# Seven products instead of eight for four pairs of f tiles of the first half, with sums on GpSimd and gated sums added by DMA

## The chip, the cores and the metric

The kernel runs on one core of a Trainium2 chip. The metric is device time in microseconds of one execution, the median of several runs. Beside it stands one profiled execution with its trace. The engines are named as in the profile: PE is the matmul engine and PEld its weight loads, DVE the vector engine, ACT the scalar engine, POOL is GpSimd, SP issues most DMAs. Each engine takes its instructions in the order of its own list; an instruction that waits for another engine holds up what stands behind it in the same list.

## The reference

A token matrix x (2048 x 512) goes through two branches that a gate mixes:

```python
g = sigmoid((x * gate_w).sum(-1, keepdims=True))
a = irfft2(rfft2(x) * (w_r + 1j * w_i))            # 2048 x 512, filter in the frequency domain
h = gelu(x @ w1 + b1)                              # 512 -> 1792
b = h @ w2 + b2                                    # 1792 -> 512
return g * a + (1 - g) * b
```

All of it is fp32. The kernel gets fp32 accuracy from the fast matmul format by splitting each operand into a high and a low part: a product takes three matmuls (high x high, high x low, low x high).

## The kernel before

**Tiling.** The tokens are four groups `c` of 512, the hidden width is 14 tiles `f` of 128, the model width 4 tiles `q` of 128. Groups 0 and 1 (`CA`) are the first half, 2 and 3 (`CB`) the second.

**First half.** `mlp(p, c)` runs three passes over f, `PASS_A = 0-4, 5-9, 10-13`. For each f and group it makes `ph = w1[f] x` (L916, 12 matmuls of 512 columns: four q, three for the split), applies gelu in PSUM on ACT (L904), splits the result into `g_..h` (ACT, L466) and `g_..l` (DVE, L467), and then `down` (L961) makes, for each q, `po = w2 g`, three matmuls for each f tile. `keep` (L971) copies `po` out on ACT with the sign turned and writes it to the DRAM tensor `bacc[c]`: plainly in the first pass, with an accumulating DMA from POOL (`acc`, L407) in the later ones. Weights that are not summed are split as `h` on ACT; the low part is made as minus `h` (ACT, L472) plus an accumulating DMA of the weight (POOL, L407).

**Second half.** `fast(p)` (L1070), four passes, `PASS_B = 0-3, 4-5, 6-9, 10-13`. It takes the f tiles in pairs and the two groups together as a 2 x 2 block product, by a scheme with seven products instead of eight (seven `times` calls of six matmuls, L1090). The scheme needs sums of weight halves (`spread_w`, L1032: `sub` makes four 128x256 sums for each pair on DVE, L1051; `sums` splits the results into high and low, L1047 and L1048) and sums of token tiles (`early_x` and `spread_x`, L1006 and L1018: `less`, L994, 128x512, on DVE; `put` splits them, L990 and L991). Products go to two PSUM banks `nu` of each pair and to two banks `ux` that are held for good; copies and additions between them run on ACT (`copy`, L1096) and DVE (`plus`, L1099). Results are split and multiplied down as in the first half, with `+1.0` in `keep`.

**The end.** In the last pass of the second half, `bacc` is read back into `bb`, multiplied by gate - 1 (L1140), and subtracted on DVE from the filter branch in the tile `y` (L1144, two 128x256 for each block). `last` (L1156) then subtracts the last down product from `y` into `oB` (L1171) and sends it out; the block that closes the kernel is cut into pieces (`tail`, L1164 for the last one), so that the last DMAs are small.

**The filter branch** runs beside all this: forward transforms (`forward`, matmuls `pd` and `py`) in the first 90 us or so, butterflies and the filter product on DVE (`radix4`, L665 to L669; `filt`, L765 to L769) after them, inverse transforms (`inverse`, `pz` and `pa`) in the last 130 us. `own_rows` sends some rows of `y` through a DMA and a small matmul before the second stage of butterflies can start.

**Order.** Every step is recorded in a graph, and two tables written out by hand or by a planner set everything: `ORDER` is the order in which the steps are emitted, and so each engine's list, and `SLOTS` is the buffer slot of each tile.

Of the kernel before, what the change touches and what calls it, by code (L numbers as in the profile page):

```python
# [16 lines left out]
P = 128  # L17
# [6 lines left out]
PASS_A = (range(0, 5), range(5, 10), range(10, 14))  # L24
# [321 lines left out]
def tile_kernel(ctx: ExitStack, tc: tile.TileContext, xt, xc, w1, w2, b1, b2, x0g, wf, wrev, out, consts):  # L346
# [9 lines left out]

    vec, act, pe, sp = nc.vector, nc.scalar, nc.tensor, nc.sync

    slots = {"t2k": 7, "ttab": 3, "xhl": 8, "w": 46, "pf": 4, "pm": 4}

    whole = ("ttab", "xhl", "w", "ctab")
    g = Graph(slots)
# [20 lines left out]
    def c_act(n, psum):  # L383
        return 0.07 + 0.82e-3 * n if psum else 0.13 + 0.765e-3 * n
# [894 lines left out]
```

## Time and profile before

| | us |
|---|---|
| median of 3 runs | 365.27 (364.29 to 366.5) |
| the profiled execution | 364.17 |
| its span in the trace | 362.3 |
| POOL busy in the span | 70.6, 91 instructions |
| granted PE clock | 1.0 all through |

The span is what the trace holds of that execution; 1.9 us lie around it. In a row of a group, the two numbers behind the first bar are the busy time of all its instructions and the mean duration of one in ns; behind the second bar stands the engine's idle time just before them and what ended it. A busy PE is one that has matmuls in flight: they overlap, so the time from start to start is less than the 390 ns that a 512-column matmul lasts.

### The profile page before, as it was taken

How to read it: one execution, taken by the hardware profiler on the slowest of the kernel's cores; microseconds unless marked ns; L12 is line 12 of the kernel's file. 1: busy time of each engine (PE TensorE's matmuls, PEld its weight loads, DVE VectorE, ACT ScalarE, POOL GpSimd, SP SyncE). 2: the span in 40 equal slices, each digit the busy share in tenths (PEclk: the TensorE clock that was granted, in tenths of full speed). 3: DMA queues.
4: the chain of work that ended last, by engine and by line, in shares of the span. 5: the costliest groups of instructions: out<-in, count | busy, mean ns of one | idle time of the engine just before them, and what ended most of it. 6: DMA issues, size and time to landing. Idle time of an engine off the chain costs nothing.

```text
span 362.3 us, 5722 instructions
## 1 busy us (share of the span) xinstructions
PE 356.1 (98%) x1808; PEld 302.2 (83%) x1808; DVE 330.8 (91%) x745; ACT 253.6 (70%) x471; POOL 70.6 (19%) x91
## 2 busy tenths in 40 slices
PE   8999999999999999999999999999999999999995
PEld 6988898898877888888888888888888888888885
DVE  5969999799978999999999999979989899899994
ACT  4984688789985563348468764899999986786100
POOL 1030000111021240111224300000432222003220
PEclk9999999999999999999999999999999999999999
DMA  7999597377689899897998954445686588858787
GB/s 242 369 337 263 176 322 203 102 162 184 208 147 237 199 261 211 198 342 226 217 263 152 148 113 134 103 133 166 83 146 123 85 149 208 166 164 203 168 228 221
DMA packets 46494, 70.34 MB, mean 194 GB/s; under 512 B 5376, under 2 KB 19200, under 8 KB 46464
## 3 DMA queue, kind: packets, MB, share of 16 engines
q1 hardware_dynamic: 34592, 48.93, 41.5%
q0 software_dynamic: 11440, 20.72, 37.1%
q10 hardware_dynamic: 432, 0.33, 0.3%
q8 instruction: 14, 0.23, 0.3%
q14 instruction: 16, 0.13, 0.1%
HBM read 48.32 MB, written 19.41 MB: 187 GB/s over the span
## 4 chain that ended last, share of the span: by engine, by line
PE 85%; DMA 5%; DVE 4%; ACT 3%; SPq 1%; issue 1%; DVEq 0%
PE poB L416 21%; PE po L416 20%; PE ph L416 14%; PE ux L1090 10%; PE nu L1090 8%; PE pz L416 4%; PE pd L416 3%; PE py L416 3%; PE pa L416 3%; DMA wb1l<-in_w 2%; DMA wb1l_raw<-in_w 2%; DMA y<-ownr 1%; ACT ph L904 1%; DVE b0s L665 0%; SPq L893 0%
## 5 line engine op out<-in xcount | busy, mean ns | idle before, releaser
L904 ACT ACTIVATE ph<-ph,b1t 128x512 f32<-128x512 f32 x28 | 18.4, 656 | 17.9 <-PE ph L416 17.8
L803 ACT ACTIVATE sw<-y,al 64x512 f32<-64x512 f32 x32 | 22.9, 721 | 1.2 <-DVE y L669 0.5
L407 POOL DMA_DIRECT2D bacc<-oB x16 | 13.9, 936 | 47.1 <-ACT oB L982 46.1
L407 POOL DMA_DIRECT2D bacc<-o x16 | 15.6, 977 | 35.8 <-ACT o L982 35.5
L765 DVE TENSOR_TENSOR m<-y,wf 128x514 f32<-128x514 f32 x32 | 21.3, 691 | 0.3
L982 ACT ACTIVATE o<-po 128x512 f32<-128x512 f32 x16 | 9.5, 596 | 15.4 <-PE po L416 9.9
L416 PEld LDWEIGHTS pz<-tg,pq 128*128 128x128 f32 x128 | 17.1, 191 | 1.9 <-PE pz L416 0.4
L416 PE MATMUL pz<-tg,pq 128*128 128x128 f32 x128 | 17.8, 275 | 0.3 <-DVE v L855 0.3
L416 PE MATMUL pd<-cf,w 128*128 128x129 f32 x128 | 17.7, 274 | 0.0
L1090 PE MATMUL nu<-xf,wa0h 128*128 128x512 f32 x56 | 17.4, 392 | 0.0
L416 PE MATMUL py<-zb,tf 128*128 128x258 f32 x96 | 17.3, 297 | 0.0
L416 PEld LDWEIGHTS pd<-cf,w 128*128 128x128 f32 x128 | 16.6, 190 | 0.6
L607 DVE TENSOR_TENSOR zb<-pd,zb 128x256 fp32r<-128x256 f32 x32 | 13.1, 419 | 4.1 <-ACT zb L604 2.2
L632 ACT ACTIVATE y<-pys 64x257 f32<-64x257 f32 x32 | 13.1, 417 | 3.5 <-DVE pys L629 3.0
L810 DVE SCALAR_TENSOR_TENSOR pq<-y,al,sw 128x256 f32<-128x256 f32 x32 | 14.9, 483 | 0.6 <-ACT sw L806 0.5
L416 PEld LDWEIGHTS pa<-zb,ci 128*128 128x128 f32 x96 | 13.7, 188 | 1.4
L416 PEld LDWEIGHTS py<-zb,tf 128*128 128x128 f32 x96 | 14.1, 190 | 0.9
L416 PE MATMUL pa<-zb,ci 128*128 128x256 f32 x96 | 14.3, 281 | 0.0
L822 ACT ACTIVATE zb<-pz 128x512 fp32r<-128x512 f32 x16 | 9.4, 597 | 6.5 <-PE pz L416 6.4
L604 ACT ACTIVATE zb<-pd 128x256 fp32r<-128x256 f32 x32 | 11.2, 387 | 3.5 <-PE py L416 2.2
L823 DVE TENSOR_TENSOR zb<-pz,zb 128x512 fp32r<-128x512 f32 x16 | 11.0, 691 | 2.8 <-ACT zb L822 2.8
L574 DVE TENSOR_TENSOR w<-eo 128x256 f32<-128x256 f32 x32 | 13.1, 421 | 0.3
(700 smaller groups left out, 1279.9 us busy)
## 6 DMA issues: line engine op xcount, KB each, us to landing
wf<-in_wf SPq DMA_DIRECT2D x16, 257.0 KB, 4.9
bacc<-o POOLq DMA_DIRECT2D x16, 256.0 KB, 7.0
bacc<-oB POOLq DMA_DIRECT2D x16, 256.0 KB, 4.2
xf<-in_xt SPq DMA_DIRECT2D x14, 256.0 KB, 4.9
wr<-in_w SPq DMA_DIRECT2D x14, 256.0 KB, 5.0
tf<-tf SPq DMA_DIRECT2D x16, 192.0 KB, 5.1
bacc<-o SPq DMA_DIRECT2D x8, 256.0 KB, 3.8
bacc<-oB SPq DMA_DIRECT2D x8, 256.0 KB, 2.2
```

The lines of the kernel that those rows point to most:

```text
L407: return add("pool", 2.3 * kb / 340, 3.4, lambda: nc.gpsimd.dma_start(dst(), src(), accum_op=ALU.add), reads, writes, rank)
L416: pe.matmul(ps, w, x, start=start, stop=stop)
L574: v(lambda s=s, op=op: vec.tensor_tensor(w.ap()[:, s], eo.ap()[:, :, 0], eo.ap()[:, :, 1], op=op), 256, [eo], [(w, s)], feed)
L604: a(lambda c=c: act.activation(segs(xh, c), both(c), AF.Copy), 256, [ps[c]], [(xh, c)], 0)
L607: v(lambda c=c: vec.tensor_tensor(segs(xl, c), both(c), segs(xh, c), op=ALU.subtract), 256, [ps[c], (xh, c)], [(xl, c)], 0)
L632: a(lambda o=o, i=i: act.activation(Y[j].ap()[o:o + HP, 1], pys.ap()[i:i + HP, 1], AF.Copy), 257, [(pys, 1)], [(Y[j], 1 + k)], 0, more=0.1)
L765: v(lambda mk=mk, k=k, y=y, w=w: vec.tensor_tensor(mk.ap(), y.ap(), w.ap()[:, k:k + 1, :ND].to_broadcast([P, 2, ND]), op=ALU.mult), 514, [ ...
L803: a(lambda sw=sw, y=y, o=o, i=i: act.activation(sw.ap()[o:o + HP], y.ap()[i:i + HP, ::-1, :HD], AF.Copy, scale=al.ap()[i:i + HP, 0:1]), 51 ...
L810: v(lambda sw=sw, pq_=pq_, y=y, j=j, k=k, op=op: vec.scalar_tensor_tensor(pq_.ap()[:, k], y.ap()[:, k, :HD], al.ap()[:, 1 + j:2 + j], sw.a ...
L823: v(lambda n=n, ps=ps: vec.tensor_tensor(zl.ap()[:, :, :, n], ps.ap(), zh.ap()[:, :, :, n], op=ALU.subtract), 512, [ps, (zh, n)], [(zl, n) ...
L904: a(lambda: act.activation(ps.ap(), ps.ap(), AF.Gelu_apprx_tanh, bias=b1t.ap()[:, f:f + 1]), 600, [b1t], [ps]).table = "gelu"
L1090: pe.matmul(o.ap(), w(wi, e), FX[j].ap()[:, xi, e], start=first, stop=k == 5, skip_group_check=not start)
```

## The change

Four things are done.

- The first half's passes become 0-5, 6-9, 10-13. The first is still `mlp`. The other two are `fast_a`, which uses the seven products, now a function `products` for both halves, on the pairs (6,7), (8,9), (10,11), (12,13). For the first half three of the token operands are the tiles that are there already (`tokens`, `WHOLE`), and only four sums are made. The two PSUM banks `ux` are set up by two matmuls with a tile of zeros.
- All sums of token tiles (`less`) and of weight halves (`sub`) are made by GpSimd, 16 of 128x512 and 44 of 128x256, instead of DVE. The tokens of both halves are loaded whole; a detour of two tiles through DRAM goes.
- At the end `bb` times gate - 1 is added to `y` by an accumulating DMA, eight of them, instead of 16 subtractions on DVE; the sign in `keep` is turned for it.
- `ORDER` and `SLOTS` are new throughout; there are 42 instead of 46 slots of 2 KB and 9 instead of 8 of 8 KB.

By instructions: PE 24 fewer of 512 columns and 2 more, DVE 23 fewer, ACT 24 more, POOL 60 sums more and 4 DMAs fewer for weights and 8 more for `y`, SP as many DMAs as before.

```diff
-PASS_A = (range(0, 5), range(5, 10), range(10, 14))
+PASS_A = (range(0, 6), range(6, 10), range(10, 14))
...
 ORDER = """
-13 0 2 3 4 5 6 7 8 9 10 11 12 15 38 14 16 26 25 506 508 18 507 527 109 1 37 39 27 19 64 17 511 23 554 543 530 167 509
+15 13 0 2 3 4 5 6 7 19 8 9 10 11 12 22 14 16 25 1 26 482 27 23 484 18 24 503 17 38 192 37 483 64 39 65 541 20 552 485
...
-    slots = {"t2k": 7, "ttab": 3, "xhl": 8, "w": 46, "pf": 4, "pm": 4}
+    slots = {"t2k": 7, "ttab": 3, "xhl": 9, "w": 42, "pf": 4, "pm": 4}
...
+    def on_pool(emit, n, reads, writes):
+        return add("gp", c_pool(n), 0.2, emit, reads, writes)
...
     def less(o, x, y):
-        v(lambda: vec.tensor_tensor(o.ap(), x.ap(), y.ap(), op=ALU.subtract), 512, [x, y], [o])
+        on_pool(lambda: nc.gpsimd.tensor_tensor(o.ap(), x.ap(), y.ap(), op=ALU.subtract), 512, [x, y], [o])
...
+    def spread_x(cs, half, after=()):
+
+        raw_ = cs == CB
+        new_forms(("11", "t1", "t2", "21", "t3", "22", "t4") if raw_ else ("t1", "t2", "t3", "t4"), half)
...
+            less(b00, b01, b00)
+            put("t1", e, b00)
             less(b01, b11, b01)
             put("t3", e, b01)
+            if raw_:
+                put("22", e, b11)
+            less(b11, b11, b00)
+            put("t2", e, b11)
+            if raw_:
+                put("21", e, b10)
+            less(b10, b10, b11)
+            put("t4", e, b10)
+
+    WHOLE = {"11": (0, 0), "21": (0, 1), "22": (1, 1)}
+
+    def tokens(half, k):
+        if half == "A" and k in WHOLE:
+            c, n = WHOLE[k]
+            bs = X[CA[c]]
+            return [*bs], lambda i, e: bs[i].ap()[:, :, 2 * n + e]
+        b = FX[k]
+        return [b], lambda i, e: b.ap()[:, i, e].rearrange("p (a b) -> p a b", a=4)
...
         def sub(o, oh, x, xh, y, yh, op=ALU.subtract):
-            v(lambda: vec.tensor_tensor(o.ap()[:, H[oh]], x.ap()[:, H[xh]], y.ap()[:, H[yh]], op=op), 256, [x, y], [o])
+            on_pool(lambda: nc.gpsimd.tensor_tensor(o.ap()[:, H[oh]], x.ap()[:, H[xh]], y.ap()[:, H[yh]], op=op), 256, [x, y], [o])
...
+    def products(half, fs, late, end):
+        cs = CA if half == "A" else CB
+        G = {}
+        if not UX:
+            zero = buf("w", [P, P], F32R, "zerob", cls="zero")
+            add("vec", 0.3, 0.1, lambda: vec.memset(zero.ap().bitcast(F32), 0.0), [], [zero])
+            UX.extend(buf("pm", [P, 512], F32, f"ux{k}", pool=pp, cls=f"ux{k}") for k in range(2))
+            for x in UX:
+                m(lambda x=x: mm(x.ap(), zero.ap(), bcast(zero.ap(), 4), True, True), 512, 1, [zero], [x])
...
+    def fast_a(p):
+        fs = PASS_A[p]
+        G = products("A", fs, [], False)
+        for f in fs:
+            load_w("b", f)
+        for n, c in enumerate(CA):
...
+                down(ps, slice(None), q, fs, W, {f: G[n, f] for f in fs})
+                keep(c, q, o, ps, False, -1.0)
...
-                    for h in range(2):
-                        y = Y[c + 8 * h + 4 * (q // 2)]
-                        v(lambda b=b, y=y, h=h, q=q: vec.tensor_tensor(
-                            y.ap()[:, q % 2, :2 * P], y.ap()[:, q % 2, :2 * P], b.ap()[:, 2 * h * P:2 * (h + 1) * P], op=ALU.subtract),
-                          256, [b], [(y, q % 2)])
+                    j = c + 4 * (q // 2)
+                    acc(lambda j=j, q=q: yy.ap()[:, j::8, q % 2, :2 * P], lambda b=b: b.ap().rearrange("p (a b) -> p a b", a=2), 256,
+                        [b], [(Y[j], q % 2), (Y[j + 8], q % 2)])
...
-                        keep(c, q, o, ps, p == 0, 1.0)
+                        keep(c, q, o, ps, p == 0, -1.0)
...
-    early_x()
-    for p in range(len(PASS_A)):
-        for c in CA:
-            mlp(p, c)
+    for c in CA:
+        mlp(0, c)
+    spread_x(CA, "A")
+    for p in range(1, len(PASS_A)):
+        fast_a(p)
```

Three places in the order that this makes. First, POOL's list where the weights of the first half's second pass are prepared. Before, it holds the accumulating DMAs for the low parts of single weights:

```order
L407 DMA wa10l<-in_w 128x512
L407 DMA wa6l<-in_w 128x512
L407 DMA wa9l<-in_w 128x512
L407 DMA wa7l<-in_w 128x512
L407 DMA wa8l<-in_w 128x512
L407 DMA wb6l<-in_w 128x512
```

In the change the same place holds the sums of weight halves (`wr` are the loaded weights of a pair, `ws` the sum tile), and the DMAs stand between them:

```order
L1060 TENSOR_TENSOR wsA_1098<-wrA_495 128x256
L1060 TENSOR_TENSOR wsA_1098<-wsA_1098,wrA_629 128x256
L1060 TENSOR_TENSOR wrA_495<-wrA_629,wrA_495 128x256
L1060 TENSOR_TENSOR wrA_495<-wrA_629,wsA_1098 128x256
L417 DMA wb6l<-in_w 128x512
L417 DMA wa0lA_1204<-in_w 128x512
L417 DMA wa0lA_1259<-in_w 128x512
L1060 TENSOR_TENSOR wsA_1291<-wrA_808 128x256
L1060 TENSOR_TENSOR wsA_1291<-wsA_1291,wrA_926 128x256
```

Instructions of computing have come into a list that had DMA issues alone.

Second, POOL's list in the second half of the change, where partial results (`oB`) are accumulated into `bacc`:

```order
L417 DMA bacc_2649<-oB_23_3005 128x512
L417 DMA bacc_2649<-oB_22_3083 128x512
L1060 TENSOR_TENSOR wrB_2389<-wrB_2312,wrB_2389 128x256
L417 DMA bacc_2649<-oB_21_3113 128x512
L1060 TENSOR_TENSOR wsB_3136<-wrB_2361 128x256
L1060 TENSOR_TENSOR wrB_2389<-wrB_2312,wsB_2645 128x256
L417 DMA bacc_2649<-oB_20_3190 128x512
```

Sums of weight halves stand behind DMA issues that wait for ACT's copy of a down product.

Third, the end of DVE's list. Before:

```order
L1144 TENSOR_TENSOR y<-y,bb_3923 128x256
L1171 TENSOR_TENSOR oB_32_4168<-y,poB_320_4123 128x256
L1171 TENSOR_TENSOR oB_33_4187<-y,poB_330_4170 128x256
L1144 TENSOR_TENSOR y<-y,bb_4033 128x256
L1164 TENSOR_TENSOR oB_33_4187<-y,poB_33256_4189 128x128 x2
```

and in the change:

```order
L1205 TENSOR_TENSOR oB_30_4178<-y,poB_300_4067 128x256
L1205 TENSOR_TENSOR oB_33_4213<-y,poB_330_4195 128x256
L1205 TENSOR_TENSOR oB_31_4237<-y,poB_310_4221 128x256 x2
L1198 TENSOR_TENSOR oB_33_4213<-y,poB_33256_4206 128x128 x2
L1205 TENSOR_TENSOR oB_20_4264<-y,poB_200_4251 128x256 x2
```

The block cut into small pieces is no longer the last; a whole block, `oB_20`, comes behind it.

More of the change, by code (lines that the diff above doesn't have):

```diff
@@ L381, in c_vec, with c_pool @@
         return 0.075 + 1.042e-3 * n
+    def c_pool(n):
+        return 0.3 + 2.1e-3 * n
     def c_act(n, psum):
@@ L951, in mlp @@
             G[f] = split(f"g{c}_{f}", "w", [P, 512], ps, lambda x: x, 512, cls="g")
-        if p == len(PASS_A) - 1:
-            free[c] = G[fs[-1]][1]
         for q in range(NQ):
@@ L988, in put @@
     def put(k, e, x):
-        h, l = ((lambda i=i: FX[k].ap()[:, i, e]) for i in range(2))
+        b = FX[k]
+        h, l = ((lambda i=i: b.ap()[:, i, e]) for i in range(2))
         a(lambda: act.activation(h(), x.ap(), AF.Copy), 512, [x], [(FX[k], e)])
@@ L993, in less @@
     def less(o, x, y):
-        v(lambda: vec.tensor_tensor(o.ap(), x.ap(), y.ap(), op=ALU.subtract), 512, [x, y], [o])
-    def new_forms(ks):
-        FX.update((k, buf("xhl", [P, 2, 2, 4 * P], F32R, f"xf{k}", parts=4, cls="xf")) for k in ks)
-    def raw_x(k, n, e, tag, cls, after=()):
-        x = buf(tag, [P, 4 * P], F32, f"xb{k}{n}{e}{cls}", cls=cls)
-        dma(lambda: sp.dma_start(x.ap(), xc[CB[n], 2 * k + e]), 256, after, [x])
-        return x
-    t2s = [one(f"t2s{e}", [P, 4 * P], pool=dp) for e in range(2)]
@@ L1006, in early_x @@
-    def early_x():
-        new_forms(("11", "t1", "t2"))
-        for e in range(2):
-            b00, b01, b11 = (raw_x(k, n, e, "w", "xe") for k, n in ((0, 0), (0, 1), (1, 1)))
-            put("11", e, b00)
-            less(b01, b01, b00)
-            put("t1", e, b01)
-            less(b11, b11, b01)
-            put("t2", e, b11)
-            dma(lambda e=e, b11=b11: sp.dma_start(t2s[e].ap(), b11.ap()), 256, [b11], [t2s[e]])
-    def spread_x():
-        new_forms(("21", "t3", "22", "t4"))
-        for e in range(2):
-            b10, b11, b01 = (raw_x(k, n, e, "w", "xb", [free[CA[0]]]) for k, n in ((1, 0), (1, 1), (0, 1)))
-            t = buf("w", [P, 4 * P], F32, f"tt{e}", cls="tt")
-            dma(lambda t=t, e=e: sp.dma_start(t.ap(), t2s[e].ap()), 256, [free[CA[0]], t2s[e]], [t])
-            put("21", e, b10)
+        on_pool(lambda: nc.gpsimd.tensor_tensor(o.ap(), x.ap(), y.ap(), op=ALU.subtract), 512, [x, y], [o])
@@ new lines, in new_forms @@
+    def new_forms(ks, half):
+        FX.update((k, buf("xhl", [P, 2, 2, 4 * P], F32R, f"x{half}{k}", parts=4, cls="x" + half)) for k in ks)
+    def spread_x(cs, half, after=()):
+        raw_ = cs == CB
+        new_forms(("11", "t1", "t2", "21", "t3", "22", "t4") if raw_ else ("t1", "t2", "t3", "t4"), half)
+        for e in range(2):
+            b00, b01, b11, b10 = (buf("w", [P, 4 * P], F32, f"xb{half}{k}{n}{e}", cls="xb" + half) for k, n in ((0, 0), (0, 1), (1, 1), (1, 0)))
+            for b, k, n in ((b00, 0, 0), (b01, 0, 1), (b11, 1, 1), (b10, 1, 0)):
+                dma(lambda b=b, k=k, n=n, e=e: sp.dma_start(b.ap(), xc[cs[n], 2 * k + e]), 256, after, [b])
+            if raw_:
+                put("11", e, b00)
+            less(b00, b01, b00)
+            put("t1", e, b00)
@@ L1026, in spread_x @@
             less(b01, b11, b01)
             put("t3", e, b01)
-            put("22", e, b11)
-            less(t, b10, t)
-            put("t4", e, t)
-    def spread_w(u, late):
+            if raw_:
+                put("22", e, b11)
+            less(b11, b11, b00)
+            put("t2", e, b11)
+            if raw_:
+                put("21", e, b10)
[7 more added lines that the diff above has]
+            return [*bs], lambda i, e: bs[i].ap()[:, :, 2 * n + e]
+        b = FX[k]
+        return [b], lambda i, e: b.ap()[:, i, e].rearrange("p (a b) -> p a b", a=4)
@@ L1033, in spread_w @@
+    def spread_w(u, late, half):
         f0, f1 = 2 * u, 2 * u + 1
         H = slice(0, HD), slice(HD, D)
-        r = [buf("w", [P, D], F32, f"wr{f}", cls="wr") for f in (f0, f1)]
+        r = [buf("w", [P, D], F32, f"wr{half}{f}", cls="wr") for f in (f0, f1)]
         for x, f in zip(r, (f0, f1)):
-            dma(lambda x=x, f=f: sp.dma_start(x.ap(), w1[f]), 256, [] if u else t2s, [x])
-        ta = buf("t2k", [P, D], F32, f"ws{u}", cls="ws", parts=2)
+            dma(lambda x=x, f=f: sp.dma_start(x.ap(), w1[f]), 256, [], [x])
+        ta = buf("t2k", [P, D], F32, f"ws{half}{u}", cls="ws", parts=2)
@@ L1039, in spread_w @@
         T = {}
         def tile_(n, parts=1):
-            T[n] = buf("w", [P, D], F32R, f"wa{n}{u}", cls="wa", parts=parts)
+            T[n] = buf("w", [P, D], F32R, f"wa{n}{half}{u}", cls="wa", parts=parts)
             return T[n]
@@ L1068, in spread_w @@
                 "s3": form(("th", "tl"), 0), "s4": form(("th", "tl"), 1), "22": form(("1",), 0)}
-    def fast(p):
-        fs = PASS_B[p]
-        end = p == len(PASS_B) - 1
-        W, G = {}, {}
-        late = [] if p else [free[CA[1]]]
-        if p == 0:
-            free["X"] = [buf("pm", [P, 512], F32, f"ux{k}", pool=pp, cls=f"ux{k}") for k in range(2)]
-        X = free["X"]
+    UX = []
+    def products(half, fs, late, end):
[7 more added lines that the diff above has]
+                m(lambda x=x: mm(x.ap(), zero.ap(), bcast(zero.ap(), 4), True, True), 512, 1, [zero], [x])
+        U = UX
         for u in range(fs[0] // 2, fs[-1] // 2 + 1):
-            A = spread_w(u, late)
-            N = [buf("pf", [P, 512], F32, f"nu{u}{k}", pool=pp, cls="nu") for k in range(2)]
+            A = spread_w(u, late, half)
+            N = [buf("pf", [P, 512], F32, f"nu{half}{u}{k}", pool=pp, cls="nu") for k in range(2)]
             def times(o, i, j, start, A=A):
                 bs, w = A[i]
+                xs, x = tokens(half, j)
                 def emit():
@@ L1089, in emit @@
                             first = start and k == 0
-                            pe.matmul(o.ap(), w(wi, e), FX[j].ap()[:, xi, e], start=first, stop=k == 5, skip_group_check=not start)
+                            pe.matmul(o.ap().rearrange("p (a b) -> p a b", a=4), w(wi, e), x(xi, e), start=first, stop=k == 5, skip_group_check=not start)
                             k += 1
-                m(emit, 512, 6, [*bs, FX[j]], [o])
+                m(emit, 512, 6, [*bs, *xs], [o])
             def copy(o, i):
@@ L1101, in done @@
             def done(ps, i, n, u=u):
-                f, c = 2 * u + i, CB[n]
+                f, c = 2 * u + i, cs[n]
                 gelu(ps, f)
@@ L1110, in fast @@
             times(N[1], "s1", "t1", True)
-            copy(X[0], N[0])
-            five = buf("t2k", [P, 512], F32, f"five{u}", cls="five")
+            copy(U[0], N[0])
+            five = buf("t2k", [P, 512], F32, f"five{half}{u}", cls="five")
             copy(five, N[1])
-            times(X[0], "s2", "t2", False)
+            times(U[0], "s2", "t2", False)
             times(N[0], "12", "21", False)
             done(N[0], 0, 0)
-            copy(X[1], X[0])
-            times(X[0], "s3", "t3", False)
-            times(X[1], "s4", "22", False)
-            plus(X[1], X[1], five)
-            done(X[1], 0, 1)
-            plus(N[1], X[0], five)
-            done(N[1], 1, 1)
-            times(X[0], "22", "t4", False)
-            done(X[0], 1, 0)
+            copy(U[1], U[0])
+            times(U[0], "s3", "t3", False)
+            times(U[1], "s4", "22", False)
+            plus(U[1], U[1], five)
+            done(U[1], 0, 1)
+            plus(N[1], U[0], five)
+            done(N[1], 1, 1)
+            times(U[0], "22", "t4", False)
+            done(U[0], 1, 0)
+        return G
+    def fast_a(p):
[4 more added lines that the diff above has]
+        for n, c in enumerate(CA):
+            if p == len(PASS_A) - 1:
+                free[c] = G[n, fs[-1]][1]
+            for q in range(NQ):
+                o = buf("w", [P, 4 * P], F32, f"o{p}_{c}{q}", parts=3, cls="o")
+                ps = buf("pm", [P, 512], F32, f"po{p}_{c}{q}", pool=pp, cls="po")
+                down(ps, slice(None), q, fs, W, {f: G[n, f] for f in fs})
+                keep(c, q, o, ps, False, -1.0)
+    def fast(p):
+        fs = PASS_B[p]
+        end = p == len(PASS_B) - 1
+        late = [] if p else [free[CA[1]]]
+        G = products("B", fs, late, end)
+        W = {}
         for f in fs:
@@ L1140, in fast @@
                     v(lambda b=b, c=c: vec.scalar_tensor_tensor(b.ap(), gb.ap()[:, c], 1.0, b.ap(), op0=ALU.subtract, op1=ALU.mult),
-                      512, [gb], [b])
-                    for h in range(2):
-                        y = Y[c + 8 * h + 4 * (q // 2)]
-                        v(lambda b=b, y=y, h=h, q=q: vec.tensor_tensor(
-                            y.ap()[:, q % 2, :2 * P], y.ap()[:, q % 2, :2 * P], b.ap()[:, 2 * h * P:2 * (h + 1) * P], op=ALU.subtract),
-                          256, [b], [(y, q % 2)])
+                            512, [gb], [b])
+                    j = c + 4 * (q // 2)
+                    acc(lambda j=j, q=q: yy.ap()[:, j::8, q % 2, :2 * P], lambda b=b: b.ap().rearrange("p (a b) -> p a b", a=2), 256,
+                        [b], [(Y[j], q % 2), (Y[j + 8], q % 2)])
                 tail = end and n == 1 and q == NQ - 1
@@ L1218, in tile_kernel @@
         stage4(c)
-    spread_x()
+    spread_x(CB, "B", [free[CA[0]]])
     for p in range(len(PASS_B)):
```

194 rows, old and new, of tables (ORDER, SLOTS) are left out of this document.

## The prediction

> **What bounds the kernel now.** I read the busy shares first, then who PE waited for, then the chain that ended last.
>
> ```profile
> PE 356.1 (98%) x1808; PEld 302.2 (83%) x1808; DVE 330.8 (91%) x745; ACT 253.6 (70%) x471; POOL 70.6 (19%) x91
> ...
> PE 85%; DMA 5%; DVE 4%; ACT 3%; SPq 1%; issue 1%; DVEq 0%
> ```
>
> ```profile
> PE none L416 <- DVE zero L484: 1.1, 1, 1.1
> PE ph L416 <- DVE wa0l L896: 0.5, 1, 0.5
> PE pz L416 <- DVE v L855: 0.3, 1, 0.3
> PE ph L416 <- DVE wa0h L891: 0.3, 1, 0.3
> PE po L416 <- DMA wb1l<-in_w: 0.2, 1, 0.2
> ```
>
> PE is the bound: 98% busy, 85% of the chain, and all its waits together are 2.4 us. So a matmul less is a matmul's time less, as long as nothing else takes PE's place. The candidate is DVE at 91%. Three windows show how much room it has.
>
> ```profile
> 20.00:60.00 40.00, 39.81 (x232) 34.75 (x231) 36.41 (x103) 28.95 (x65) 3.02 (x5) 1.00 0.86 264
> 60.00:220.00 160.00, 159.86 (x756) 133.44 (x755) 150.46 (x331) 108.91 (x208) 35.70 (x41) 1.00 0.85 197
> 220.00:340.00 120.00, 119.73 (x627) 102.16 (x626) 112.29 (x237) 99.57 (x171) 24.37 (x28) 1.00 0.67 144
> ...
> 100.00:120.00 20.00, 16.28 (x32) 1.00 0.90 197
> ```
>
> The columns are length, then busy time of PE, weight loads, DVE, ACT, POOL, the granted clock (1.00), DMA share and GB/s; the last row is DVE alone. From 60 to 220 us, where the first half's second and third pass and the filter run, PE has no gap worth naming and DVE is free for 160 - 150.5 = 9.5 us. Of these, 3.7 us lie in 100 to 120 us, where the butterflies wait for rows that come back by DMA; in an in-order queue they can't be filled at will. From 220 to 340 us 7.7 us are free.
>
> **Matmuls.** The chain gives the price of one 512-column matmul inside a run of them.
>
> ```profile
> 158.31 8.16 PE ph L416 x36
> ```
>
> 8.16 / 36 = 0.227 us. Four pairs of f tiles took 2 x 2 x 12 = 48 matmuls each and now take 7 x 6 = 42: 24 fewer, -5.4 us. Two matmuls with zeros that set up the two sums in PSUM add 0.45. Together **-5.0 us**, on the path.
>
> The two sums hold two of four banks from the first half on, so the down products have two left. That is the arrangement that the second half has now, where PE shows no wait beyond 0.3 us; I cost it at nothing.
>
> **DVE.** What it gains and loses, by rows:
>
> ```profile
> L1144 DVE TENSOR_TENSOR y<-y,bb 128x256 f32<-128x256 f32 x16 | 6.6, 423 | 0.0
> L560 DVE TENSOR_TENSOR mxl<-xf,mxh 128x512 fp32r<-128x512 f32 x8 | 5.5, 688 | 0.1
> L1099 DVE TENSOR_TENSOR nu<-ux,five 128x512 f32<-128x512 f32 x7 | 4.9, 696 | 0.5 <-PE ux L1090 0.5
> L1099 DVE TENSOR_TENSOR ux<-ux,five 128x512 f32<-128x512 f32 x7 | 4.9, 695 | 0.0
> L1048 DVE TENSOR_TENSOR wasl<-ws,wash 128x512 fp32r<-128x512 f32 x7 | 4.8, 690 | 0.4 <-ACT wash L1047 0.4
> L1051 DVE TENSOR_TENSOR wr<-wr,ws 128x256 f32<-128x256 f32 x7 | 3.0, 423 | 0.0
> L1057 DVE TENSOR_TENSOR wa<-wr,wa 128x256 fp32r<-128x256 f32 x7 | 2.9, 421 | 0.3 <-ACT wa L1056 0.3
> ```
>
> It loses 28 weight half sums (28 x 0.42 = 11.8), 8 token sums (8 x 0.69 = 5.5) and the 16 subtractions at the end (6.6): 23.9 us. It gains for the first half 8 additions from PSUM (5.6), 8 low parts of weight sums (5.5), 4 of the last form (1.7) and 8 low parts of token forms (5.5): 18.3 us. Over the whole kernel that is 5.6 us less, but not where it is needed: all 18.3 us belong to the first half, before about 180 us, while there only 13 half sums and 4 token sums leave (5.5 + 2.8 = 8.3). So the stage from 60 to 220 us gets some 10 us more, against 9.5 free, of which 5.8 are usable. Between 0 (filter work is put off past 220 us, where the change makes room) and 10 - 5.8 = 4.2 us reach PE; I take the middle, **+2 us**.
>
> ACT's list grows by 24 instructions, none longer than this one:
>
> ```profile
> L1047 ACT ACTIVATE wash<-ws 128x512 fp32r<-128x512 f32 x7 | 4.4, 629 | 0.8 <-DMA bacc<-oB 0.7
> ```
>
> At most 24 x 0.63 = 15 us, in a stage where ACT has 160 - 108.9 = 51 us free: nothing. In the first window, where the 8 token sums of the first half fall, DVE has 3.6 us free and PE was busy 39.8 of 40.
>
> **GpSimd's sums** are the disputed term: 16 of 128x512 and 44 of 128x256. The trace has no instruction in which this engine reads SBUF, so neither their length nor what they do to DVE is shown. Length: not under what DVE takes for the same (0.69 and 0.42 us); as the far end I take the slowest pass over 512 elements in the trace and POOL's own DMA issue.
>
> ```profile
> L1199 ACT ACTIVATE gb<-gt 128x512 f32<-128x512 f32 x4 | 4.4, 1110 | 0.0
> ...
> L407 POOL DMA_DIRECT2D bacc<-oB x16 | 13.9, 936 | 47.1 <-ACT oB L982 46.1 <-PE pz L416 1.0
> ```
>
> By the order, 34 half sums and 8 token sums stand between the first pair of the first half and the fourth of the second, the full stage: 34 x 0.42 + 8 x 0.69 = 19.8 us to 34 x 0.94 + 8 x 1.11 = 40.8 us. No row is nearer to one end; I take 30. Read alone, 30 us in 160 leave POOL's queue, at 35.7 us, far from full. The question is whether DVE goes on beside them. Most of its work there reads two operands from SBUF, as the sums do:
>
> ```profile
> L467 DVE TENSOR_TENSOR g_7l<-ph,g_7h 128x512 fp32r<-128x512 f32 x2 | 1.4, 692 | 0.3 <-ACT g_7h L466 0.3
> ...
> L765 DVE TENSOR_TENSOR m<-y,wf 128x514 f32<-128x514 f32 x32 | 21.3, 691 | 0.3
> ```
>
> What reads PSUM is the splits like the first row (nine f tiles x 1.4) and the additions of L1099, now more of them; the products and butterflies, like the second row, do not. I put the share that reads SBUF twice at three quarters. If a sum stops such an instruction for its own length, DVE loses 0.75 x 30 = 22.5 us in a stage where it has none to spare, and its order is fixed, so PE's operands (the low parts) come late by as much. If the two run freely, it loses nothing. With no row between, I take half: **+11.3 us** (ends 0 and 0.75 x 40.8 = 30.6). The remaining 18 sums fall where DVE has 3.6 and 7.7 us free, and I cost them at nothing.
>
> The Trainium skill (SBUF — State Buffer, "Who interferes with whom") has a rule for this: a VectorE instruction with two SBUF inputs and a GpSimd instruction that reads SBUF use one shared interface, and the second to start is blocked until the first has finished. By it the term would be the whole 22.5 us and the time 386; no run so far shows it. The skill (GPSIMD Engine Reference, "Elementwise — side-by-side cycle accounting") gives 4497 ns for a two-input add of 2048 elements; my estimate from that page, 1.12 and 0.56 us, would make the 42 sums 28 us.
>
> **The end.**
>
> ```profile
> 357.11 0.42 DVE L1171 TENSOR_TENSOR oB<-y,poB 128x256 f32<-128x256 f32 x1 [0.22 <-PE poB L416]
> 357.45 0.42 DVE L1144 TENSOR_TENSOR y<-y,bb 128x256 f32<-128x256 f32 x1
> 358.55 0.48 DVE L1164 TENSOR_TENSOR oB<-y,poB 128x128 f32<-128x128 f32 x2 [0.68 <-PE poB L416]
> ...
> w<-ba POOLq DMA_DIRECT2D x8, 256.0 KB, 4.1
> out<-oB SPq DMA_DIRECT2D x7, 256.0 KB, 3.7
> ```
>
> Now two half-size pieces close the kernel: 0.48 us of DVE, then 362.3 - 359.03 = 3.27 us to the end. The change computes a full block last: two times 0.42 and then 256 KB in 3.7: 4.5 against 3.75, **+0.8 us**. The subtractions of L1144 become accumulating DMAs, 0.94 us to issue and 4.1 to land like the ones into w. The tightest (bb32) has 16 DVE instructions, about 9 us, between its factor and its use; if these were gone, up to 5 us would show.
>
> **Sum**, against the profiled execution (364.2): -5.0 + 2 + 11.3 + 0.8 = +9.1, so 373.3; the median of the three runs lies 1.1 above that execution, hence **374 us**. The ends: no holding and no DVE shortage 364.2 - 4.2 + 1.1 = 361; all held at the long price 364.2 - 5.0 + 4.2 + 30.6 + 0.8 + 1.1 = 396.
>
> **Rivals.** First, GpSimd and DVE don't disturb each other and the filter work slides behind 220 us: 361 us. For it speaks that POOL is idle 81% of the span and DVE's total falls by 5.6 us; against it that DVE is full just where the sums run. Second, no holding, but DVE's 4.2 us reach PE: -5.0 + 4.2 + 0.8 is nothing, 365 us. Third, on the slower side whatever DVE does: POOL's queue is late.
>
> ```profile
> POOL bacc L407 <- ACT oB L982: 46.1, 12, 14.5
> POOL bacc L407 <- ACT o L982: 35.5, 10, 7.9
> ```
>
> POOL stood still up to 14.5 us before a write of partial results, and nobody cared, since only other DMAs were behind it. Now half sums stand behind such issues, and behind the sums ACT's high part, DVE's low part and the matmuls of `ux` and `nu`. One such wait, the 7.9 us one, that isn't covered by an early place gives -5.0 + 7.9 + 0.8 = +3.7, so 369 us; it decides once a sum is issued less than its wait ahead of its product.
>
> **How the numbers follow.** Holding 0.50 (365 to 396, likeliest 374); undisturbed 0.26; DVE full without holding 0.10; a late queue 0.14. A measurement of this kernel tells 0.5%, 1.8 us, from no change. Undisturbed is faster (0.26), the second rival is the same (0.10), holding and the late queue are slower (0.64). The range has to take in the undisturbed case, for its 0.26, and leaves out the far end of the holding: 360.5 to 388. Holding alone: 366 to 390.
>
> **What would show it.** Right: DVE instructions with two SBUF inputs that are longer, or stand idle, beside a sum, and PE waits for `g_..l`, `wasl` or `watl` between 60 and 220 us that add up to over 10 us; matmul time down by 5 us all the same. Wrong: DVE durations of 0.69 and 0.42 unchanged beside the sums, or PE waits still under 3 us. PE waits that begin at a POOL instruction would speak for the late queue; a gap only after 355 us would mean that the end was mis-sized.

## The result, and the profile after

The changed kernel takes 392.78 us (median of 4 runs, 390.88 to 394.32) against 365.03 us before: ratio 1.075, 95% interval 1.069 to 1.081. The prediction was 374 us with a range up to 388, slower with a chance of 0.64. The side was right, the size was not: the time lies above the range.

The busy shares of the profiled execution after (span 390.8 us), and the shares of the chain that ended last:

```profile
PE 362.3 (93%) x1786; PEld 298.0 (76%) x1786; DVE 358.9 (92%) x722; ACT 264.5 (68%) x495; POOL 149.1 (38%) x155
...
PE 39%; DVE 29%; issue 10%; ACT 8%; DMA 7%; POOL 5%; SPq 0%; DVEq 0%; POOLq 0%; ACTq 0%
```

VectorE has 23 instructions fewer than before and is busy for 28.1 us more; the span grew by 28.5 us. PE was 85% of the chain and is 39%. By windows (length, then busy time of PE, weight loads, VectorE, ScalarE, GpSimd, the granted clock, DMA share and GB/s):

```profile
20.00:60.00 40.00, 39.82 (x220) 34.07 (x218) 33.73 (x89) 23.68 (x53) 13.13 (x12) 1.00 0.75 193
60.00:220.00 160.00, 146.27 (x681) 118.46 (x680) 156.34 (x304) 115.80 (x228) 72.36 (x71) 0.98 0.77 185
220.00:340.00 120.00, 112.32 (x539) 90.28 (x538) 114.19 (x209) 91.53 (x158) 46.06 (x47) 1.00 0.71 137
```

VectorE is now full from 60 to 220 us (156.3 of 160) and nearly so to 340, and PE, which had gaps of 0.1 and 0.3 us there, is idle for 13.7 and 7.7 us. What PE waited for, longest first:

```profile
PE ux L1104 <- DVE waslB L1057: 5.1, 1, 5.1
PE po L426 <- DVE g_12l L477: 1.9, 2, 1.1
PE ux L1104 <- DVE xBt L1000: 1.8, 1, 1.8
PE ux L1104 <- DVE nuB L1113: 1.8, 2, 1.5
PE pz L426 <- DVE tg L807: 1.8, 2, 1.3
```

These five of 21 rows name VectorE, and so does most of the rest: its rows come to 19 of 24 us. Only one wait is long: VectorE is late in many places, by a little. Why, its groups by shape tell (count, busy us, mean ns):

```profile
L775 DVE TENSOR_TENSOR m<-y,wf 128x514 f32<-128x514 f32 x32 | 25.2, 803 | 0.0
L584 DVE TENSOR_TENSOR w<-eo 128x256 f32<-128x256 f32 x32 | 14.8, 484 | 0.4 <-PE po L426 0.2
L617 DVE TENSOR_TENSOR zb<-pd,zb 128x256 fp32r<-128x256 f32 x32 | 13.1, 416 | 0.9 <-ACT zb L614 0.7
...
L1000 DVE TENSOR_TENSOR xBt<-xbB,xBt 128x512 fp32r<-128x512 f32 x8 | 7.4, 941 | 0.4 <-ACT xBt L999 0.4
...
L1113 DVE TENSOR_TENSOR ux<-ux,fiveB 128x512 f32<-128x512 f32 x7 | 4.8, 688 | 0.0
```

The filter's products `m` took 691 ns on average before and take 803; low parts of tokens (`xBt`, the same kind of instruction as `mxl`, which took 688) take 941. But the two rows with an operand in PSUM (`pd`, `ux`) stand at 416 and 688 ns, as before (417 and 695). The timeline shows one such place, VectorE first and GpSimd below (start us, us):

```profile
183.98 1.16 DVE L1000 TENSOR_TENSOR xB<-xbB,xB 128x512 fp32r<-128x512 f32 x1
185.07 2.93 DVE L775 TENSOR_TENSOR m<-y,wf 128x514 f32<-128x514 f32 x2
187.92 3.27 DVE L1000 TENSOR_TENSOR xBt<-xbB,xBt 128x512 fp32r<-128x512 f32 x2
191.12 0.68 DVE L775 TENSOR_TENSOR m<-y,wf 128x514 f32<-128x514 f32 x1
```

```profile
184.56 1.18 POOL L1060 TENSOR_TENSOR wsB<-wrB 128x256 f32<-128x256 f32 x1
185.70 1.75 POOL L1003 TENSOR_TENSOR xbB<-xbB,xbB 128x512 f32<-128x512 f32 x1
187.39 0.86 POOL L417 DMA_DIRECT2D bacc<-o  x1
188.01 1.02 POOL L1060 TENSOR_TENSOR wsB<-wsB,wrB 128x256 f32<-128x256 f32 x1
```

Two products that take 1.28 us together elsewhere (a row of the last section) take 2.93 us while two sums run. Counted over the whole trace, 138 VectorE instructions ran beside a sum. 103 of them read SBUF twice; 43 of these were more than 0.08 us longer than usual for their shape, by 31.9 us in sum and up to 1.7 us each. Of the 35 that had PSUM as an operand, none was longer. Away from the sums no instruction was longer at all. I call this the holding. (Beside a sum means that the two overlap in time.)

### The profile page after: what moved, and what is told of

It is laid out like the page before. It is cut to its first block, busy times and chain, and to the rows that moved or that the text cites. A ratio compares the mean times of both kernels' runs of the same rounds, so it can differ in the third digit from the quotient of the medians.

```text
span 390.8 us, 5821 instructions
## 1 busy us (share of the span) xinstructions
PE 362.3 (93%) x1786; PEld 298.0 (76%) x1786; DVE 358.9 (92%) x722; ACT 264.5 (68%) x495; POOL 149.1 (38%) x155
## 4 chain that ended last, share of the span: by engine, by line
PE 39%; DVE 29%; issue 10%; ACT 8%; DMA 7%; POOL 5%; SPq 0%; DVEq 0%; POOLq 0%; ACTq 0%
PE po L426 9%; PE ph L426 7%; PE poB L426 7%; PE ux L1104 6%; DMA bacc<-oB 4%; DVE m L775 2%; PE pd L426 2%; PE nuA L1104 2%; POOL wsB L1060 2%; PE pz L426 2%; PE nuB L1104 2%; DVE y L679 2%; DMA wa0lB<-in_w 1%; DVE y L677 1%; DVE xBt L1000 1%
## 5 line engine op out<-in xcount | busy, mean ns | idle before, releaser
L775 DVE TENSOR_TENSOR m<-y,wf 128x514 f32<-128x514 f32 x32 | 25.2, 803 | 0.0
L1003 POOL TENSOR_TENSOR xbA<-xbA,xbA 128x512 f32<-128x512 f32 x8 | 11.2, 1409 | 23.5 <-DVE pys L639 16.0
L1104 PE MATMUL nuB<-xB,wa0hB 128*128 128x512 f32 x56 | 17.9, 401 | 1.0 <-ACT ux L1110 0.5
L914 ACT ACTIVATE ux<-ux,b1t 128x512 f32<-128x512 f32 x22 | 14.5, 657 | 4.8 <-PE ux L1104 4.7
L1060 POOL TENSOR_TENSOR wsB<-wrB 128x256 f32<-128x256 f32 x7 | 12.2, 1737 | 10.7 <-DVE b3s L679 7.9
L1003 POOL TENSOR_TENSOR xbB<-xbB,xbB 128x512 f32<-128x512 f32 x8 | 12.7, 1588 | 8.4 <-DVE xB L1000 4.2
L584 DVE TENSOR_TENSOR w<-eo 128x256 f32<-128x256 f32 x32 | 14.8, 484 | 0.4 <-PE po L426 0.2
L581 DVE TENSOR_TENSOR eo<-xf 128x256 f32<-128x256 f32 x32 | 13.9, 456 | 1.3 <-ACT y L642 1.3
L426 PEld LDWEIGHTS pa<-zb,ci 128*128 128x128 f32 x96 | 12.7, 188 | 3.2 <-DVE zb L833 1.3
L914 ACT ACTIVATE nuB<-nuB,b1t 128x512 f32<-128x512 f32 x14 | 9.2, 660 | 8.2 <-DVE nuB L1113 7.5
```

The costliest lines, as they stand in the source:

```text
L426: pe.matmul(ps, w, x, start=start, stop=stop)
L581: v(lambda s=s, op=op: vec.tensor_tensor(eo.ap()[:, s], x.ap()[:, 0:2], x.ap()[:, 2:4], op=op), 256, [x], [(eo, s)], feed)
L584: v(lambda s=s, op=op: vec.tensor_tensor(w.ap()[:, s], eo.ap()[:, :, 0], eo.ap()[:, :, 1], op=op), 256, [eo], [(w, s)], feed)
L775: v(lambda mk=mk, k=k, y=y, w=w: vec.tensor_tensor(mk.ap(), y.ap(), w.ap()[:, k:k + 1, :ND].to_broadcast([P, 2, ND]), op=ALU.mult), 514, [ ...
L914: a(lambda: act.activation(ps.ap(), ps.ap(), AF.Gelu_apprx_tanh, bias=b1t.ap()[:, f:f + 1]), 600, [b1t], [ps]).table = "gelu"
L1003: on_pool(lambda: nc.gpsimd.tensor_tensor(o.ap(), x.ap(), y.ap(), op=ALU.subtract), 512, [x, y], [o])
```

## The experiments

Three theories stood against each other: the holding (1); the new order, the two PSUM banks held or the DMA subtractions (2); a late GpSimd queue (3). Each kernel was timed beside the kernel before on the same chip; the experiments used three chips, so those from different chips are best compared by their ratios.

**Short sums.** The steps and the order stay; each sum is cut to 8 columns, so most of it is left out. For the token sums, in `less`:

```diff
-        on_pool(lambda: nc.gpsimd.tensor_tensor(o.ap(), x.ap(), y.ap(), op=ALU.subtract), 512, [x, y], [o])
+        on_pool(lambda: nc.gpsimd.tensor_tensor(o.ap()[:, :8], x.ap()[:, :8], y.ap()[:, :8], op=ALU.subtract), 512, [x, y], [o])
```

and the same for each half sum in `sub`, whose readers repeat the 8 columns.

> All 60 sums on GpSimd work on 8 columns instead of 512 or 256 (what reads the sums repeats these 8 columns, so most of each sum is left out); steps, order, buffers, matmuls, VectorE's own instructions and every wait on a sum stay. Theory 1 (a sum that reads SBUF holds VectorE's instructions with two SBUF inputs: the 43 of them that were longer by 31.9 us in sum): VectorE's busy time falls from 358.9 to about 327 us, no such instruction is longer, and PE is the bound again: 360 to 366 us. Theory 2 (the loss is in the new order, the two PSUM banks held, or the subtractions made by DMA): the sums' length does not matter, 380 to 393 us. Theory 3 (GpSimd's queue is late because it waits for its DMA issues' inputs): those waits stay, 375 to 390 us.

> As above, but only the 44 half sums of weights are short; the 16 sums of tokens are whole. In the changed kernel's trace 19.3 us of the lengthening lie beside half sums. Theory 1: VectorE's busy time about 339 us and the time 392.8 - 19.3 = 373.5, so 370 to 377 us. Theory 2: 385 to 393. Theory 3: 380 to 392.

> Only the 16 sums of tokens are short (8 columns); the 44 half sums of weights are whole. In the changed kernel's trace 11.4 to 12.4 us of the lengthening lie beside sums of tokens, which the prediction had partly costed at nothing. Theory 1: VectorE's busy time about 347 us, the time 378 to 384 us. Theory 2: 388 to 393. Theory 3: within 2 us of the changed kernel where the queue stands behind a DMA issue, 388 to 393.

Measured: all short 367.72 us (ratio 1.0053, 1.0019 to 1.0086); half sums short 377.83 us (1.035, 1.029 to 1.041); token sums short 382.41 us (1.049, 1.044 to 1.054). The page and the windows with all sums short:

```profile
PE 355.7 (98%) x1786; PEld 297.1 (81%) x1786; DVE 325.5 (89%) x722; ACT 263.9 (72%) x495; POOL 109.2 (30%) x155
```

```profile
60.00:220.00 160.00, 158.75 (x754) 131.18 (x753) 154.76 (x338) 124.86 (x243) 57.02 (x76) 1.00 0.84 200
220.00:340.00 120.00, 117.59 (x605) 97.37 (x603) 109.68 (x224) 98.04 (x169) 37.75 (x49) 1.00 0.82 162
```

The same 722 VectorE instructions are busy for 33.4 us less, none of the 90 that read SBUF twice beside a sum is longer, and PE is the bound again. The length of the sums is worth 392.8 - 367.7 = 25.1 us, all that it does to VectorE, PE and GpSimd's own queue together, and its parts add up: 15.0 for the half sums, 10.4 for the token sums. By theory 1 the first lies 1.7 us above the range, which ended at 366, and the second 0.8 above 377, and the third is inside; all three lie outside the ranges of theories 2 and 3.

**Sums on VectorE.** `nc.gpsimd` becomes `vec` in `less` and `sub`.

> All 60 sums are done by VectorE, at the same places of the order; nothing is left out. VectorE gets 16 x 0.69 + 44 x 0.42 = 29.5 us of work of its own and loses 31.9 us of holding. Theory 1: hardly a change, 386 to 395 us, with no VectorE instruction longer than before; GpSimd as a helper saved nothing. Theory 2: about the same, 385 to 395, so this run does not tell 1 from 2. Theory 3 (late queue): the sums no longer stand behind GpSimd's DMA issues, below 378 us.

Measured: 380.77 us (1.044, 1.039 to 1.048), which no theory had.

```profile
PE 360.5 (95%) x1786; PEld 298.2 (79%) x1786; DVE 348.4 (92%) x782; ACT 264.4 (70%) x495; POOL 76.0 (20%) x95
```

VectorE does all 60 sums itself and is busy for 10.5 us less than when GpSimd did them. Against short sums they cost it 348.4 - 325.5 = 22.9 us; as GpSimd's they cost it 33.4. My 29.5 us was too much chiefly because successive VectorE instructions overlap by 0.08 us (in the timeline above, 185.07 + 2.93 is 188.00, and the next starts at 187.92), which is some 5 us for 60. So the helper took more of VectorE's time than its help was worth. It also says what the scheme takes without any holding when VectorE makes the sums: still 15 us more than the kernel before.

**What in a sum holds.** The same 60 places, filled with zeros in one kernel and with a copy of one input in another; the sums are left out. In `less` (`sub` likewise):

```diff
-        on_pool(lambda: nc.gpsimd.tensor_tensor(o.ap(), x.ap(), y.ap(), op=ALU.subtract), 512, [x, y], [o])
+        on_pool(lambda: nc.gpsimd.memset(o.ap(), 0.0), 512, [x, y], [o])
```

```diff
-        on_pool(lambda: nc.gpsimd.tensor_tensor(o.ap(), x.ap(), y.ap(), op=ALU.subtract), 512, [x, y], [o])
+        on_pool(lambda: nc.gpsimd.tensor_copy(o.ap(), (y if o is x else x).ap()), 512, [x, y], [o])
```

> Each of the 60 sums becomes a fill with zeros of the same 512 or 256 columns on GpSimd: it writes the same place at the same point of the order but reads nothing (the sums themselves are left out). Theory 1 (GpSimd's reading of SBUF holds VectorE): no VectorE instruction is longer beside a fill, busy time about 325 us, 364 to 371 us as with short sums. Theory 1b (any long GpSimd instruction on SBUF holds VectorE, its writing too): instructions are longer beside fills and the time is above 375 us.

> Each of the 60 sums becomes a GpSimd copy of one of its inputs, same length: one SBUF input instead of two (the sums are left out). Theory 1 (reading SBUF at all is enough): VectorE instructions with two SBUF inputs are longer beside the copies, by as much as the copies are long, 376 to 393 us. Theory 1c (it needs two SBUF inputs on GpSimd's side as on VectorE's): none is longer, 364 to 371 us.

Measured: fills 366.16 us (1.0035, 0.9997 to 1.0072); copies 373.77 us (1.023, 1.017 to 1.029). The filter's products with the fills, then with the copies:

```profile
L775 DVE TENSOR_TENSOR m<-y,wf 128x514 f32<-128x514 f32 x32 | 21.3, 684 | 0.0
...
L1003 POOL MEMSET xbB<- 128x512 f32 x8 | 4.8, 606 | 7.4 <-DVE wf L770 3.8 <-DVE xB L1000 3.6
```

```profile
L775 DVE TENSOR_TENSOR m<-y,wf 128x514 f32<-128x514 f32 x32 | 23.0, 735 | 0.0
```

Beside fills of 0.61 us no VectorE instruction is longer (0 of 68 that read SBUF twice). Beside copies 34 of 103 are, by 8.9 us in sum, and none of 35 with a PSUM operand. Reading SBUF holds, with one input too; writing does not. A copy of 512 columns takes from 0.61 us and a sum from 1.27, so less holding is no surprise; the time lies below the range that I gave for it (376 to 393) and above the one for no holding (364 to 371). This is the rule of the Trainium skill (SBUF — State Buffer, "Who interferes with whom") that the prediction weighed: a two-SBUF-input VectorE instruction contends with a GpSimd instruction that reads SBUF, not with one that only writes it. The runs agree on both halves.

**GpSimd's sums without the rest.** The kernel before with `nc.gpsimd` for `vec` in its own `less` and `sub`.

> The kernel before with nothing but its 8 sums of tokens and 28 half sums moved from VectorE to GpSimd, same order. VectorE loses 8 x 0.60 + 28 x 0.335 = 14.2 us of occupied time. Theory 1: it gets more back as holding, by the changed kernel's rows (second half: 14.9 + 7.5 + 1.0 = 23.4 us), so its busy time rises by about 9 us to 340 and the time to 368 to 376 us. Rival (no holding worth naming without the rest of the change): VectorE's busy time falls to about 317 us and the time is that of before within 0.5%, since PE is the bound.

Measured: 376.69 us (1.032, 1.027 to 1.038).

```profile
PE 359.4 (96%) x1808; PEld 303.1 (81%) x1808; DVE 335.7 (90%) x709; ACT 254.4 (68%) x471; POOL 104.2 (28%) x127
```

VectorE lost 36 instructions and is busy for 4.9 us more: 20 instructions are longer by 19.5 us, 4.9 of them in a single one (shown in the last section), against an estimated 14.2 us of work that left (335.7 = 330.8 - 14.2 + 19.5, within 0.4). The holding needs nothing of the rest of the change. The time is a little above the expected range, so that 36 sums on GpSimd cost this kernel 12 us.

**Cut sums.** Each sum as four instructions of a quarter of its columns, here in `less`:

```diff
-        on_pool(lambda: nc.gpsimd.tensor_tensor(o.ap(), x.ap(), y.ap(), op=ALU.subtract), 512, [x, y], [o])
+        def four():
+            for k in range(4):
+                s = slice(k * P, k * P + P)
+                nc.gpsimd.tensor_tensor(o.ap()[:, s], x.ap()[:, s], y.ap()[:, s], op=ALU.subtract)
+
+        on_pool(four, 512, [x, y], [o])
```

> The changed kernel with each sum on GpSimd cut into four instructions of a quarter of its columns; nothing is left out. Theory 1 with holding by the whole time that GpSimd reads: the pieces read as many columns, plus a fixed cost for 180 more instructions, so VectorE is held as long or longer and the time is 388 to 410 us; each single lengthening is shorter (below 0.6 us instead of up to 1.7). Rival (VectorE slips in between the pieces and loses a quarter at most): 372 to 380 us.

Measured: 390.80 us (1.071, 1.062 to 1.079); held in sum 25.7 us over 111 instructions. VectorE does not slip through at a quarter of the price: the holding fell by a fifth, the time hardly. That each lengthening would be below 0.6 us was wrong: the longest was 2.2 us, in an instruction that stood still beside eight pieces of two sums in a row.

**The end, and the rest.** Short sums again, with the gated sums added to `y` by VectorE:

```diff
-                    acc(lambda j=j, q=q: yy.ap()[:, j::8, q % 2, :2 * P], lambda b=b: b.ap().rearrange("p (a b) -> p a b", a=2), 256,
-                        [b], [(Y[j], q % 2), (Y[j + 8], q % 2)])
+                    v(lambda j=j, q=q, b=b: vec.tensor_tensor(yy.ap()[:, j::8, q % 2, :2 * P], yy.ap()[:, j::8, q % 2, :2 * P], b.ap().rearrange("p (a b) -> p a b", a=2), op=ALU.add), 512,
+                        [b, (Y[j], q % 2), (Y[j + 8], q % 2)], [(Y[j], q % 2), (Y[j + 8], q % 2)])
```

> Short sums (8 columns) as in the first run of this kind, and the 8 accumulating DMAs that add the gated sums into y at the end are 8 additions of 512 elements on VectorE again. If adding by DMA costs nothing, as predicted: the same as with short sums alone, 365 to 370 us, or up to 2 us more where VectorE is full after 330 us. If the DMAs or the place in GpSimd's queue cost something: 1 to 4 us less than with short sums alone.

Measured: 371.56 us (1.017, 1.012 to 1.023), against 1.0053 with the DMAs: some 4 us more, and above both ranges. With short sums the DMAs are worth that much in this order; with whole sums it was not measured.

And short sums with the seven copies `five` of the second half on VectorE:

```diff
-            copy(five, N[1])
+            if half == "B":
+                v(lambda five=five, N=N: vec.tensor_copy(five.ap(), N[1].ap()), 512, [N[1]], [five])
+            else:
+                copy(five, N[1])
```

> Short sums (8 columns) and, for the seven pairs of the second half, the copy of a product out of PSUM (the one that VectorE then adds) made by VectorE instead of ScalarE. With short sums PE still stood 6.8 us more between matmuls than in the kernel before: 2.5 us of that between 100 and 220 us, 3.7 us between 220 and 300 us, where ScalarE runs without a gap from 252 to 284 us and VectorE has 6 us free of 40. If ScalarE is what PE waits for there: PE's gaps from 220 to 300 us fall by 2 us or more, time 364 to 366.5 us. If not: gaps as before or longer, 367 to 370 us.

Measured: 369.88 us (1.013, 1.008 to 1.019). PE's gaps from 220 to 300 us went from 5.7 to 4.8 us, not by 2, and others grew. Easing ScalarE at VectorE's cost does not remove what PE waits for there; as VectorE got the work, ScalarE's part in it is not settled.

None of these versions beat the kernel before. Even with sums of almost no length, or with fills in their place, the scheme in this order is not faster than it, so a better way of summing alone would not have made it faster.

## Why the prediction was right or wrong

- **Matmuls, -5.0: right.** The intervals between the starts of successive matmuls (the last one's own length included), with all that exceeds the median of their shape left out, come to 347.0 us before and 342.2 after: -4.8. What exceeds it went from 10.5 to 43.2 us; that is where the time went.
- **VectorE's own work, +2, and the rest of the order.** With short sums that excess is 17.3 us, 6.8 more than before: 2.5 of it between 100 and 220 us, which is the step as I put it, and 4.0 between 220 and 300 us (3.7 in the last expectation), which I had at nothing. Why PE stands there is open: the one remedy tried (ScalarE's copies on VectorE) did not help.
- **PSUM banks, nothing: right as far as seen.** PE's longest wait for ScalarE to empty a bank of the down products was 1.0 us in the changed kernel's trace.
- **ScalarE's 24 instructions, nothing:** not refuted; no run took them out.
- **GpSimd's sums, +11.3: the step that failed.** The mechanism was the one named, the size was 25.1 us. Besides the length (next point), two choices made it small. I took half of "held whole" because no row stood between the ends, though the Trainium skill's rule (SBUF — State Buffer, "Who interferes with whom") is not one of degree. And I costed 18 of the sums at nothing, in windows where VectorE had 3.6 and 7.7 us free. In the trace 17.3 us of the holding lie between 60 and 220 us, 3.6 before and 10.9 behind: nearly half outside the stage that I priced. All 60 sums, at the shortest that each shape takes, last 16 x 1.27 + 44 x 0.73 = 52 us, and the 31.9 us of holding are six tenths of that; I had put three eighths (half of three quarters) on 30 us. A priced loss has to be set against the free time of its window, and 10.9 us don't fit into 7.7, of which most belongs to waits that come where they come.
- **Length of a sum.** The shortest sums of the two shapes take 1.27 and 0.73 us in this trace; my bounds were 0.69 to 1.11 and 0.42 to 0.94, so the far end was too near for 512 columns. My estimate from the Trainium skill (GPSIMD Engine Reference, "Elementwise — side-by-side cycle accounting"), 1.12 and 0.56, was short too.

Their rows, with GpSimd's own waiting for VectorE in the means:

```profile
L1003 POOL TENSOR_TENSOR xbB<-xbB,xbB 128x512 f32<-128x512 f32 x8 | 12.7, 1588 | 8.4 <-DVE xB L1000 4.2 <-PE po L426 3.4 <-DMA xbB<-in_xc 0.8
...
L1060 POOL TENSOR_TENSOR wsA<-wrA 128x256 f32<-128x256 f32 x4 | 3.3, 816 | 18.5 <-DVE w L584 12.4 <-DVE y L677 6.1
```

- **The end, +0.8: +0.5.** From the last matmul's end to the end of the span it was 3.8 us and is 4.3.
- **The additions to `y` by DMA, nothing:** they hid, as predicted, and with short sums they saved 4 us that I had not credited, because I took VectorE's relief after 330 us as not needed.
- **The rivals.** The undisturbed and the VectorE-full case fell with the longer instructions. The late queue is not the main loss: PE's waits name no GpSimd instruction, and with the sums off GpSimd's queue the time was 380.8, not below 378. In the longest wait of PE, 5.1 us for `waslB`, ScalarE had made the high part by 189.7 us, and VectorE's list came to the low part at 197.9. But ScalarE did wait for GpSimd's sums (7.9 us for `wrB`, 4.1 for `xbB`), so lateness is not excluded as a part of the 12 us between 392.8 and 380.8.
- **The signs that I named.** VectorE's longer instructions came. The waits of PE for `g_..l`, `wasl` and `watl` between 60 and 220 us came to 7.0 us, not to over 10; all its waits for VectorE there were 11.5 us, the rest for a token form, the gate and the filter branch. I had looked for the loss in too few tiles.

The sum with measured terms: 365.4 - 4.8 + 6.8 + 25.1 + 0.5 = 393.0, against 392.8, where 365.4 is the kernel before as timed beside the short sums. As 25.1 is itself the difference to the short sums, what this tests is only the rest: 2.5 us from the three other terms, 2.3 measured.

## What to carry to other kernels

A GpSimd instruction that reads SBUF is no free help beside a VectorE queue of two-operand work from SBUF: here 60 sums cost VectorE 33 us as GpSimd's and 23 us as its own. What these runs show as free of holding is GpSimd work beside VectorE instructions with a PSUM operand (0 of 35 longer), and fills (0 of 68). When a rule says that one of two instructions stops, price it whole, as one end of the range, for every place where it applies, and set each place against the free time of its own window. Read a slowdown first from instruction durations by shape: a busy time that rises while the count falls asks whether the same shapes have become longer.

## What the hardware showed that was not expected

- The holding goes both ways, and it can last for several instructions of the other engine. Beside back-to-back VectorE instructions one half sum took 4.35 us instead of 0.73, and with sums of 8 columns single ones took from 0.19 to 3.8 us. The first, with VectorE at its usual pace; it ended at 238.51, together with the first VectorE instruction in this stretch that has a PSUM operand (`g_3l`):

```profile
234.16 4.35 POOL L1060 TENSOR_TENSOR wsB<-wsB,wrB 128x256 f32<-128x256 f32 x1
```

```profile
235.08 1.28 DVE L775 TENSOR_TENSOR m<-y,wf 128x514 f32<-128x514 f32 x2
...
237.22 0.68 DVE L775 TENSOR_TENSOR m<-y,wf 128x514 f32<-128x514 f32 x1
237.83 0.68 DVE L477 TENSOR_TENSOR g_3l<-nuB,g_3h 128x512 fp32r<-128x512 f32 x1
```

  The other way round, in the kernel before with GpSimd's sums, a VectorE instruction that takes 0.16 us elsewhere stood beside four sums and ended with the last of them. PE then waited 2.3 us for VectorE's next instruction:

```profile
162.78 5.08 DVE L760 SCALAR_TENSOR_TENSOR wf<-wf,rev 128x4 f32<-128x4 f32 x1
```

```profile
162.55 1.60 POOL L994 TENSOR_TENSOR tt<-xb101xb,tt 128x512 f32<-128x512 f32 x1
163.99 1.40 POOL L994 TENSOR_TENSOR xb011xb<-xb111xb,xb011xb 128x512 f32<-128x512 f32 x1
165.23 1.38 POOL L994 TENSOR_TENSOR tt<-xb100xb,tt 128x512 f32<-128x512 f32 x1
166.47 1.36 POOL L994 TENSOR_TENSOR xb010xb<-xb110xb,xb010xb 128x512 f32<-128x512 f32 x1
```

- An instruction's size does not protect it: the 16 of 128x4 elements on `wf` took 163 ns on average before and 432 after.

```profile
L760 DVE SCALAR_TENSOR_TENSOR wf<-wf,rev 128x4 f32<-128x4 f32 x16 | 2.5, 163 | 0.0
...
L770 DVE SCALAR_TENSOR_TENSOR wf<-wf,rev 128x4 f32<-128x4 f32 x16 | 6.7, 432 | 0.0
```

- Where PE stood longest, the granted clock fell too, so a wait cost more than itself. After the wait of 5.1 us, eleven matmuls of 512 columns started 0.43 to 0.60 us apart instead of 0.227, which is some 2.4 us more. The clock was 0.5 from 196.7 to 203.5 us. In the twelve traces, each of the nine waits of PE of 2.3 us and more has such a stretch beside it (3.4 us long in the other eight), and no wait of 1.8 us or less has one of its own; the one other stretch before PE's last matmul lies at 7.6 us in the trace with fills, where PE is still starting. The window before, then after:

```profile
180.00:220.00 40.00, 40.00 (x178) 33.13 (x177) 38.74 (x80) 27.93 (x52) 11.54 (x14) 1.00 0.86 175
...
180.00:220.00 40.00, 31.03 (x123) 24.21 (x123) 39.12 (x65) 24.20 (x45) 28.37 (x27) 0.91 0.89 191
```
